# Output projection with u^T stationary and the Wo columns moving, tokens on PSUM rows

## The chip, the cores and the metric

The kernel runs on one core of a Trainium2 chip. Its time is the device time of one execution in microseconds, the median over runs. The engines named below are TensorE (PE, with its weight loads listed apart as PEld), VectorE (DVE), ScalarE (ACT), GpSimd (POOL) and SyncE (SP). SP issues the loads of weights; ACT computes and also issues all other DMAs. Each engine works through its own list of instructions in order.

## The reference

Two branches share the input x (2048 tokens of 640) and are mixed by a gate per token. Branch B is a gated feed-forward layer. Branch A is attention with a recurrent memory: the tokens come in 64 segments of 32, eight memory rows are put ahead of each, and the attention output at the memory rows is the memory of the next segment.

```python
for s in range(n_seg):                       # 64 segments of 32 tokens
    xs = x[:, s * seg_len:(s + 1) * seg_len, :]
    h = jnp.concatenate([mem, xs], axis=1)   # 8 memory rows + 32 tokens
    q, k, v = (einsum('btd,dhe->bhte', h, W) for W in (Wq, Wk, Wv))   # 32 heads of 192
    scores = where(mask, einsum('bhqe,bhke->bhqk', q, k) * scale, -1e9)
    p = softmax(scores)                      # memory rows see all, tokens are causal
    o = einsum('bhqk,bhke->bhqe', p, v)
    o = einsum('bhte,hed->btd', o, Wo)       # the output projection
    mem = o[:, :M, :]
    outs.append(o[:, M:, :])
out = g * a + (1 - g) * b                    # g = sigmoid((x * gate_w).sum(-1))
```

The chain from one segment's memory to the next cannot be broken: Q, K and V of a segment need the memory that the segment before leaves.

## The kernel before

The program is written in Bass. Every operation is put in by `S_.add` with the regions that it reads and writes; from them a small planner works out the semaphore waits (a PSUM bank is one region). The order on each engine is the order of the calls.

Three phases come one after the other. First the feed-forward branch: its rows, already multiplied by 1 - g, are stored to a scratch in HBM (`b_scr`), x is stored transposed (`xts`), and the gates lie in `gcol`, 128 tokens on the partitions and one column for each group of four segments. Then the "left" phase: Q and K of the last eight tokens of every segment, which don't need the memory, are computed for all segments at once and put into a scratch, since 40 rows don't fit into 32. Then the 64 segments, one after the other.

A segment follows the list `PROG` (L463): for each of four octets of heads Q (`q`, `cmode`, L915), its transposition on DVE (`tq`), K, V (`v_oct`, L932), scores (`sc`, L955), softmax (`ex`, L988), transposition of p (`pt`, `p_transp`, L1006), PV (`pv`, `pv_oct`, L1021) and output projection (`wo`, `wo_part`, L1053), interleaved so that TensorE has work while ACT and DVE are at the softmax. In Q, K and V 32 rows (8 memory, 24 tokens) are stationary, in four column tiles of 32, and 384 weight columns move through each. In the output projection it is the other way round: each 128x128 block of Wo is stationary and the 40 columns of u^T move, 48 chunks x 5 blocks = 240 matmuls per segment, all summed up in PSUM bank 7 (`OB`). The result stands transposed: model columns on the partitions and tokens along the row.

What follows on it, at the end of `segment` (L1106 to L1116): ACT copies the eight memory columns into `Hb`, from where the next segment's Q, K and V read them (L1111), and two DVE copies put the other 32 columns into `aT4` (L1113, L1115). After four segments `out_group` (L894) turns `aT4` back by five transposes, mixes it with the rows of branch B in `rowb`, loaded from `b_scr` (L1085), and `out_store` (L902) writes 128 rows.

The weights of branch A, 84 pieces of 384 KB (Wq, Wk, Wv) or 320 KB (Wo), don't all fit into SBUF. As many as fit are resident; two are held in unused corners of PSUM and copied out by ACT (`held2_copy`, L592; `held_copy`, L600); the others are streamed again in every segment through a ring of five slots (`issue_ring`, L546). How many are streamed follows from the bytes that are left (L503 to L511): it is 21. SP issues a streamed piece as soon as the slot that it takes is free.

The names to keep: L920 is the matmul of Q and K, L939 of V, L960 of the mask, L968 of the scores, L1010 and L1011 of `pt`, L1030 to L1042 of PV, L1062 of the output projection, L896 the transposes of `out_group` and L898 its mix. `aux_dma` (L662) is the helper that issues DMAs on ACT.

Of the kernel before, what the change touches and what calls it, by code (L numbers as in the profile page):

```python
# [3 lines left out]
ACTF = mybir.ActivationFunctionType  # L4
# [217 lines left out]
def _build(nc, A_x, A_mem0, A_Wq, A_Wk, A_Wv, A_Wo, seg_len, w_gate, w_up, w_down,  # L222
# [55 lines left out]
    wsA["small"] = al(NG * 4 + 8 + 32 + 16)  # L278
    wsA["ident"] = al(128 * 2)
    wsA["maskm"] = al(R * 2)  # L280
    wsA["rowb"] = al(Dm * 2)
# [12 lines left out]
    wsB["aT4"] = al(KT * 128 * 2)  # L294
# [54 lines left out]
    for k, n in (("gcol", 0), ("mbd", 4 * NG), ("mle", 4 * NG + 8), ("gwT", 4 * NG + 40)):  # L349
        wsA_off[k] = wsA_off["small"] + n  # L350
# [7 lines left out]
    gcol = fview(wsA_off["gcol"], 4 * NG)  # L358
    r_gcol = sreg(wsA_off["gcol"], 4 * NG)
# [15 lines left out]
    rowb = bview(wsA_off["rowb"], Dm * 2)  # L375
    r_rowb = sreg(wsA_off["rowb"], Dm * 2)
# [20 lines left out]
    PTl = bview(wsB_off["PTl"], 256).rearrange("p (i t r) -> p i t r", t=4, r=16)  # L397
# [7 lines left out]
    aT4 = bview(wsB_off["aT4"], KT * 256).rearrange("p (k t) -> p k t", t=128)  # L405
    r_aT4 = sreg(wsB_off["aT4"], KT * 256)
    mem0r = rowb
    r_mem0r = r_rowb
# [178 lines left out]
    HB2 = ((5, 0, 480, 528), (6, 480, 960, 528), (7, 960, 1536, 432))  # L587
# [61 lines left out]
    asel(maskm[:, 0:XA], r_maskm, [[-1, XA]], 0, 1, NEG)  # L649
    asel(maskm[:, L:R], r_maskm, [[-1, M]], -L, 1, NEG)  # L650
    asel(maskm[:, L:R], r_maskm, [[0, M]], -L, 1, 0.0)
    asel(maskm[:, L:R], r_maskm, [[0, M]], -XA, 1, NEG)
# [51 lines left out]

    def chain_init():
        pv7 = psb(7)
        S_.add("pe", [lambda e, k=k: e.transpose(pv7[:, k * M:(k + 1) * M], mem0r[0:M, k * 128:(k + 1) * 128], ident[0:M, 0:M])
                      for k in range(KT)],
               reads=[r_mem0r, r_ident], writes=[r_ps[7]], name="mem0T")
        x_load(0)  # L710
        S_.add("act", lambda e: e.activation(out=Hb[0][:, :, XA:L], in_=pv7[:, 0:KT * M].rearrange("p (k m) -> p k m", m=M),
                                             func=ACTF.Copy),
               reads=[r_ps[7]], writes=[r_Hm[0]], name="mem0T evac")

    def x_load(s):
        nb = s % 2
        aux_dma(Hb[nb].rearrange("p k r -> p (k r)"), xts[s], [Rg("xt", s, s + 1)], [r_Hm[nb], r_Hxp[nb]], "xl")
# [176 lines left out]
    def out_group(g, bk):  # L894
        pv = psb(bk)
        S_.add("pe", [lambda e, k=k: e.transpose(pv[:, k * 128:(k + 1) * 128], aT4[:, k, :], ident) for k in range(KT)],  # L896
               reads=[r_aT4, r_ident], writes=[r_ps[bk]], name="aT transp g%d" % g)
        S_.add("dve", lambda e: e.scalar_tensor_tensor(out=rowb, in0=pv[:, 0:Dm], scalar=gcol[:, g:g + 1], in1=rowb,  # L898
                                                       op0=ALU.mult, op1=ALU.add),
               reads=[r_ps[bk], r_rowb, r_gcol], writes=[r_rowb], name="mix g%d" % g)  # L900

    def out_store(g):  # L902
        aux_dma(out2[128 * g:128 * g + 128, :], rowb, [r_rowb], [], "outw", True)

# [101 lines left out]
    def p_transp(s, o):  # L1006
        bank = 5 + o % 2
        q = s % 4
        pv = psb(bank)
        S_.add("pe", [lambda e: e.transpose(pv[:, 320:424], pm_sb[0:104].rearrange("p t k -> p (t k)"), ident[0:104, 0:104]),  # L1010
                      lambda e: e.transpose(pv[:, 424:528], pl_sb[0:104].rearrange("p t k -> p (t k)"), ident[0:104, 0:104])],  # L1011
               reads=[r_p, r_ident], writes=[r_ps[bank]], name="pT s%d o%d" % (s, o))
        S_.add("dve", lambda e: e.tensor_tensor(  # L1013
            out=PTm, in0=apx(pv[:, 320:424], [[64, 2], [0, 4], [1, R]]), in1=apx(mbd, [[0, 2], [1, 4], [0, R]]),
            op=ALU.mult), reads=[r_ps[bank], r_mbd], writes=[r_PTm], name="pT evac s%d o%d" % (s, o))
        S_.add("dve", lambda e: e.tensor_tensor(  # L1016
            out=PTl, in0=apx(pv[:, 424 + XA:528], [[64, 2], [0, 4], [1, 16]]),
            in1=apx(mle[:, q, :], [[0, 2], [1, 4], [0, 16]]),
            op=ALU.mult), reads=[r_ps[bank], r_mle], writes=[r_PTl], name="pTl evac s%d o%d" % (s, o))

    def pv_oct(s, o):  # L1021
        A, B = misc_bank(), misc_bank()
        v, vl, u = v_sb[o % NVB], vl_sb[o], uT[o % NUB]
        ru = r_uTp[o % NUB]

        def pair(bank, c0, ncol, e0, ia, ib):
            full = ps[:, bank, c0:c0 + ncol]
            n = ib - ia
            part = full.rearrange("p (i t r) -> p i t r", t=4, r=R)[:, :, :, XA:R]
            return [lambda e: e.matmul(full, v[:, e0:e0 + 128], PTm[:, ia:ib], start=True, stop=False,  # L1030
                                       skip_group_check=True),
                    lambda e: e.matmul(part, vl[:, e0:e0 + 128], PTl[:, ia:ib], start=False, stop=True,  # L1032
                                       skip_group_check=True)]

        W = 4 * R
        S_.add("pe", pair(A, 0, W, 0, 0, 1) + pair(A, W, W, 256, 1, 2),
               reads=[r_v[o % NVB], r_vl[o], r_PTm, r_PTl], writes=[r_ps[A]], name="PVa s%d o%d" % (s, o))
        fns = []
        for lhs, pt, left in ((v, PTm, False), (vl, PTl, True)):
            for h in range(2):  # L1040
                dst = ps[64 * h:64 * h + 64, B, 0:W].rearrange("p (t r) -> p t r", r=R)
                fns.append(lambda e, lhs=lhs, pt=pt, left=left, h=h, dst=dst[:, :, XA:R] if left else dst: e.matmul(  # L1042
                    dst, lhs[:, 128 + 64 * h:192 + 64 * h], pt[:, h], start=not left, stop=left,
                    tile_position=(0, 64 * h), skip_group_check=True))
        S_.add("pe", fns, reads=[r_v[o % NVB], r_vl[o], r_PTm, r_PTl], writes=[r_ps[B]], name="PVb s%d o%d" % (s, o))
        S_.add("act", lambda e: e.activation(  # L1046
            out=apx(u[:, 0, 0, :], [[2 * R, 2], [3 * R, 4], [1, R]]),
            in_=ps[:, A, 0:2 * W].rearrange("p (c t r) -> p c t r", t=4, r=R), func=ACTF.Copy),
            reads=[r_ps[A]], writes=[ru[0]], name="uT evac s%d o%d" % (s, o))
        S_.add("dve", lambda e: e.tensor_copy(out=u[:, :, 1, :], in_=ps[:, B, 0:W].rearrange("p (t r) -> p t r", r=R)),  # L1050
               reads=[r_ps[B]], writes=[ru[1]], name="uT mid s%d o%d" % (s, o))

    def wo_part(s, item):  # L1053
        for p in wo_pairs(item):
# [3 lines left out]
            for i in range(2):  # L1058
                c = 2 * p + i
                tl, cc = divmod(c % 12, 3)  # L1060
                for n in range(KT):
                    fns.append(lambda e, g_=g_, i=i, c=c, n=n, tl=tl, cc=cc, u=u: e.matmul(  # L1062
                        ps[:, OB, n * R:(n + 1) * R], g_[:, i, n * 128:(n + 1) * 128], u[:, tl, cc, :],
                        start=(c == 0 and n == 0), stop=(c == NCH - 1), skip_group_check=True))
            S_.add("pe", fns, reads=[rg_, r_uT[(p // WOP) % NUB]], writes=[r_ps[OB]], name="Wo s%d p%d" % (s, p))

    def segment(s):
        g, q = s // 4, s % 4
        for item in PROG:
            kind, i = item[0], item[1]  # L1070
            if kind in ("q", "k"):
# [4 lines left out]
                if kind == "k" and i == 0 and q == 0 and g > 0:  # L1076
                    out_group(g - 1, misc_bank())
                if kind == "k" and i == 1:
                    if q == 0 and g > 0:
                        out_store(g - 1)  # L1080
                if kind == "k" and i == 2:
                    if q == 3:
                        if g + 1 < NG:
                            xleft_load(g + 1)
                        aux_dma(rowb, b_scr[128 * g:128 * g + 128, :], [Rg("dr", 128 * g, 128 * g + 128)], [r_rowb], "rowb")  # L1085
# [22 lines left out]
        O3 = ps[:, OB, 0:KT * R].rearrange("p (n r) -> p n r", r=R)  # L1108
        if s + 1 < NSEG:
            nb = (s + 1) % 2  # L1110
            S_.add("act", lambda e: e.activation(out=Hb[nb][:, :, XA:L], in_=O3[:, :, XA:L], func=ACTF.Copy),  # L1111
                   reads=[r_ps[OB]], writes=[r_Hm[nb]], name="mem evac s%d" % s)
        S_.add("dve", lambda e: e.tensor_copy(out=aT4[:, :, q * L:q * L + XA], in_=O3[:, :, 0:XA]),  # L1113
               reads=[r_ps[OB]], writes=[r_aT4], name="aT evac s%d" % s)
        S_.add("dve", lambda e: e.tensor_copy(out=aT4[:, :, q * L + XA:(q + 1) * L], in_=O3[:, :, L:R]),  # L1115
               reads=[r_ps[OB]], writes=[r_aT4], name="aT evac2 s%d" % s)  # L1116

    xleft_load(0)
# [4 lines left out]
    out_group(NG - 1, misc_bank())  # L1123
    out_store(NG - 1)
# [79 lines left out]
```

## Time and profile before

Time: 1969.43 us, the median of 3 runs (1960.42 to 1974.47). The profiled execution has a span of 1987.3 us.

| what | per run |
|---|---|
| TensorE busy | 1801.4 us (91%), 41036 matmuls |
| weight loads busy | 1179.6 us (59%) |
| DVE busy | 1025.4 us (52%) |
| ACT busy | 813.0 us (41%) |
| POOL busy | 144.7 us (7%) |
| output projection, L1062 | 15360 matmuls of 40 columns |
| Q and K, L920 | 10240 matmuls of 384 columns, in four column tiles |
| V, L939 | 6400 matmuls of 384 columns, in four column tiles |
| DMA | 577.49 MB, mean 291 GB/s |
| weight loads by DMA | 528 of Wo, 404 of Wk, 341 of Wq, 146 of Wv, about 5 us each from issue to landing |
| stores of out | 16 of 160 KB |

The first six slices of the span are the feed-forward branch and the left phase, the rest are the segments. Busy times of TensorE overlap, since the ends of matmuls are modelled: what a stretch of matmuls costs is read from the distance of the starts, not from the mean of one. "Idle before" names what ended an engine's wait, and "issue" stands for time in which it waited for nothing that the profile shows.

### The profile page before, as it was taken

What the parts mean: (1) busy time and instruction counts of PE and PEld (TensorE: products, weight loads), DVE (VectorE), ACT (ScalarE), POOL (GpSimd) and SP (SyncE); (2) the same over time, 40 slices, a digit from 0 to 9 for tenths busy, and PEclk for the clock granted to TensorE, in tenths of its full rate; (3) what the DMA queues carried; (4) which work ended last, traced back from release to release, by engine and by line L of the source; (5) the groups of instructions that cost most, each with busy time, mean ns of one, the idle gap of its engine ahead of it and who ended that gap; (6) DMA issues with size and microseconds to landing.
All of it is one profiled execution on the core that took longest, in us unless ns stands there. A gap on an engine that the chain in (4) does not pass through costs nothing.

```text
span 1987.3 us, 92275 instructions
## 1 busy us (share of the span) xinstructions
PE 1801.4 (91%) x41036; PEld 1179.6 (59%) x41044; DVE 1025.4 (52%) x3164; ACT 813.0 (41%) x1980; POOL 144.7 (7%) x546
## 2 busy tenths in 40 slices
PE   7899996999989999998999899989898999999898
PEld 3454443666666666666666666666665566666665
DVE  3222232555555556565555465555565555555555
ACT  2222221444444444444444444444444444444443
POOL 1000000000000000000000000000000000000000
PEclk9999996999999999999999999999999999999999
DMA  9411569999999999999999999999999999999998
GB/s 372 161 44 64 132 152 331 319 312 316 322 314 315 297 328 314 324 318 313 318 328 317 302 319 335 301 321 312 314 303 306 305 312 321 308 316 325 315 315 283
DMA packets 348330, 577.49 MB, mean 291 GB/s; under 512 B 79506, under 2 KB 232602, under 8 KB 347930
## 3 DMA queue, kind: packets, MB, share of 16 engines
q1 hardware_dynamic: 276922, 531.99, 79.7%
q10 hardware_dynamic: 71008, 39.60, 7.2%
q8 instruction: 320, 5.24, 1.1%
q14 instruction: 80, 0.66, 0.1%
HBM read 550.38 MB, written 21.10 MB: 288 GB/s over the span
## 4 chain that ended last, share of the span: by engine, by line
PE 65%; DMA 26%; issue 4%; ACT 2%; DVE 2%; ACTq 1%; SPq 0%; DVEq 0%
PE ps L920 17%; PE ps L1062 16%; PE ps L939 10%; DMA arena<-in_A_Wq_dram 8%; DMA arena<-in_A_Wo_dram 8%; DMA arena<-in_A_Wk_dram 5%; PE ps L831 5%; DMA arena<-in_A_Wv_dram 3%; PE ps L764 3%; PE ps L761 3%; PE ps L968 3%; PE ps L1042 2%; PE ps L779 2%; PE ps L1030 2%; PE ps L960 1%
## 5 line engine op out<-in xcount | busy, mean ns | idle before, releaser
L920 PE MATMUL ps<-arena 128*32 128x384 bf16 x10240 | 546.2, 335 | 75.7 <-DMA arena<-in_A_Wq_dram 22.5
L1062 PE MATMUL ps<-arena 128*128 128x40 bf16 x15360 | 442.3, 180 | 57.0 <-issue 41.4
L1062 PEld LDWEIGHTS ps<-arena 128*128 128x128 bf16 x15360 | 413.1, 96 | 78.8 <-issue 47.1
L920 PEld LDWEIGHTS ps<-arena 128*32 128x32 bf16 x10240 | 255.0, 98 | 264.6 <-DMA arena<-in_A_Wq_dram 53.3
L924 ACT ACTIVATE arena<-ps 128x384 bf16<-128x384 f32 x512 | 251.4, 491 | 314.6 <-PE ps L920 276.5
L929 DVE STREAM_TRANSPOSE arena<-arena 128x384 bf16<-128x384 bf16 x512 | 292.2, 571 | 115.7 <-ACT arena L924 115.6
L939 PE MATMUL ps<-arena 128*32 128x384 bf16 x6400 | 325.1, 332 | 10.8 <-DMA arena<-in_A_Wv_dram 7.3
L939 PEld LDWEIGHTS ps<-arena 128*32 128x32 bf16 x6400 | 161.7, 98 | 112.8 <-DMA arena<-in_A_Wv_dram 15.1
L950 ACT ACTIVATE arena<-ps 128x384 bf16<-128x384 f32 x256 | 125.7, 491 | 150.3 <-PE ps L939 145.6
L889 POOL COPY arena<-arena 128x96 bf16<-128x96 bf16 x256 | 68.4, 267 | 1628.7 <-PE ps L968 854.1
L1013 DVE TENSOR_TENSOR arena<-ps,arena 128x320 bf16<-128x320 bf16 x256 | 125.2, 489 | 56.0 <-PE ps L1011 50.9
L1046 ACT ACTIVATE arena<-ps 128x320 bf16<-128x320 f32 x256 | 111.6, 436 | 98.3 <-PE ps L1032 97.9
L1113 DVE CAST arena<-ps 128x120 bf16<-128x120 f32 x64 | 18.1, 283 | 256.2 <-ACT arena L1111 252.5
L997 DVE TENSOR_REDUCE arena<-ps 104x4 f32<-104x160 f32 x256 | 81.9, 320 | 123.8 <-ACT ps L995 123.0
L968 PE MATMUL ps<-arena 128*40 128x40 bf16 (+1 forms) x4096 | 120.4, 181 | 1.7 <-issue 0.8
L594 ACT ACTIVATE arena<-ps 128x480 bf16<-128x480 bf16 (+1 forms) x192 | 113.9, 593 | 18.7 <-PE ps L861 16.6
L607 ACT ACTIVATE arena<-ps 128x256 bf16<-128x256 bf16 x320 | 103.7, 386 | 42.2 <-DVE arena L1016 10.9
L983 DVE TENSOR_REDUCE arena<-ps 104x4 f32<-104x160 f32 x256 | 81.2, 317 | 63.0 <-PE ps L968 62.8
L1111 ACT ACTIVATE arena<-ps 128x40 bf16<-128x40 f32 x63 | 12.9, 204 | 246.1 <-PE ps L1062 246.1
L1050 DVE CAST arena<-ps 128x160 bf16<-128x160 f32 x256 | 77.7, 303 | 59.4 <-PE ps L1042 59.1
L968 PEld LDWEIGHTS ps<-arena 128*40 128x40 bf16 (+1 forms) x4096 | 99.7, 96 | 12.6 <-DVE arena L929 1.3
L831 PE MATMUL ps<-arena 128*128 128x512 bf16 x480 | 104.2, 379 | 1.2 <-ACT arena L838 1.2
(75 smaller groups left out, 1712.8 us busy)
## 6 DMA issues: line engine op xcount, KB each, us to landing
arena<-in_A_Wo_dram SPq DMA_DIRECT2D x528, 320.0 KB, 4.8
arena<-in_A_Wk_dram SPq DMA_DIRECT2D x404, 384.0 KB, 5.1
arena<-in_A_Wq_dram SPq DMA_DIRECT2D x341, 384.0 KB, 5.0
arena<-in_A_Wv_dram SPq DMA_DIRECT2D x146, 384.0 KB, 5.1
left_qk_scratch<-arena ACTq DMA_DIRECT2D x16, 768.0 KB, 8.1
arena<-left_qk_scratch ACTq DMA_DIRECT2D x64, 192.0 KB, 4.9
arena<-in_A_x_dram SPq DMA_DIRECT2D x4, 640.0 KB, 15.2
xt_scratch<-arena ACTq DMA_DIRECT2D x4, 640.0 KB, 9.0
```

The costliest lines, as they stand in the source:

```text
L594: S_.add("act", lambda e: e.activation(out=bview(o_held2, GQ)[:, c0:c1], in_=psb(b)[:, p0:p0 + c1 - c0], func=ACTF.Copy), reads=[r_ps[b]], ...
L607: S_.add("act", lambda e, b=b: e.activation(out=flat[:, 256 * b:256 * b + 256], in_=psb(b)[:, 768:1024], func=ACTF.Copy), reads=[r_ps[b]], ...
L831: S_.add("pe", [lambda e, k=k, g_=gs[k][0], i=i, bk=bk: e.matmul(ps[:, bk, 0:NL].rearrange("p (g t) -> p g t", t=L), g_[:, i * 128:(i + 1) ...
L920: S_.add("pe", [lambda e, j=j, k=k, gv=gv: e.matmul(ps[32 * j:32 * j + 32, bank, 0:384].rearrange("p (c i) -> p c i", i=32), Hb[hb][:, k, ...
L924: S_.add("act", lambda e: e.activation(out=rows_sb[m], in_=ps[:, bank, 0:384], func=ACTF.Copy), reads=[r_ps[bank]], writes=[r_rows[m]], na ...
L929: S_.add("dve", lambda e: e.transpose(out=dst[:, :, 0:L], in_=rows_sb[m].rearrange("p (c r) -> p c r", r=L)), reads=[r_rows[m]], writes=[r ...
L939: return [lambda e, j=j: e.matmul(ps[32 * j:32 * j + 32, bk, 0:384], lhs, g_[:, 384 * j:384 * (j + 1)], start=(k == 0), stop=(k == KT - 1) ...
L950: S_.add("act", lambda e: e.activation(out=v_sb[o % NVB], in_=ps[:, bank, 0:384], func=ACTF.Copy), reads=[r_ps[bank]], writes=[r_v[o % NVB ...
L968: fns.append(lambda e, gp=gp, lo=lo, hi=hi, i=3 * tl + c, tl=tl, last=(c == 1): e.matmul(ps[gp:gp + R, bank, tl * R:(tl + 1) * R], Qs[lo:h ...
L1013: S_.add("dve", lambda e: e.tensor_tensor(out=PTm, in0=apx(pv[:, 320:424], [[64, 2], [0, 4], [1, R]]), in1=apx(mbd, [[0, 2], [1, 4], [0, R]]),
L1046: S_.add("act", lambda e: e.activation(out=apx(u[:, 0, 0, :], [[2 * R, 2], [3 * R, 4], [1, R]]), in_=ps[:, A, 0:2 * W].rearrange("p (c t r ...
L1062: fns.append(lambda e, g_=g_, i=i, c=c, n=n, tl=tl, cc=cc, u=u: e.matmul(ps[:, OB, n * R:(n + 1) * R], g_[:, i, n * 128:(n + 1) * 128], u[ ...
```

## The change

The output projection is turned: u^T (128x40) becomes stationary, and Wo moves. Each chunk takes two matmuls of 320 columns, one for each half of the 640 model columns; the halves go to two column tiles of 64, partitions 0 to 39 and 64 to 103 of bank 7. 96 matmuls per segment take the place of 240, and the result stands with tokens on the rows, as `out` and `b_scr` have them. So the transposes of `out_group` and `aT4` go, and each segment is mixed and stored by itself: the gates are spread to a column per segment (`gate_spread`, `gseg`), the rows of B come by two loads per segment (`b_load`), one mix works on both halves, and two stores write it (`out_store`).

The memory, though, is needed with model columns on the partitions. So DVE copies the rows out of PSUM (`mrow`), six small matmuls turn the eight memory rows back (stationary: a piece of `mrow`; moving: eight columns of the identity), and DVE copies the result into `Hb`. The tokens' order in a segment changes with it: the memory comes first, then 24 tokens, then the left eight, so that the 32 tokens are contiguous rows. The mask, the left part of PV (`PTl`) and the load of x (`x_load`) follow this order. The regions of PSUM that hold a weight piece move out of bank 7's first 320 columns (`HB2`), and the transposed p goes to the start of its bank.

```diff
-    wsA["small"] = al(NG * 4 + 8 + 32 + 16)
+    wsA["small"] = al(NSEG * 4 + 8 + 32 + 16)
+    HD = Dm // 2
-    wsA["rowb"] = al(Dm * 2)
+    wsA["rowb"] = al(HD * 2)
+    wsA["mrow"] = al(HD * 2)
-    wsB["aT4"] = al(KT * 128 * 2)
...
-    HB2 = ((5, 0, 480, 528), (6, 480, 960, 528), (7, 960, 1536, 432))
+    HB2 = ((5, 0, 576, 320), (6, 576, 1152, 320), (7, 1152, 1536, 640))
...
+    def gate_spread():
+        S_.add("pool", [lambda e: e.memset(gseg, 0.0), lambda e: e.memset(rowb, 0.0), lambda e: e.memset(mrow, 0.0)],
+               writes=[r_gseg, r_rowb, r_mrow], name="gate zero")
+        for i in range(8):
+            q, h = i % 4, i // 4
+            aux_dma(gseg[64 * h + M:64 * h + R, NG * q:NG * q + NG], gcol[L * q:L * q + L, :], [r_gcol],
+                    [sreg(wsA_off["gseg"] + 8 * i, 8)], "gl%d" % i)
...
-        aux_dma(Hb[nb].rearrange("p k r -> p (k r)"), xts[s], ...
+        aux_dma(Hb[nb].rearrange("p k r -> p (k r)")[:, M:KT * L], xts[s][:, 0:KT * L - M], ...
...
-    def out_group(g, bk):
-        pv = psb(bk)
-        S_.add("pe", [lambda e, k=k: e.transpose(pv[:, k * 128:(k + 1) * 128], aT4[:, k, :], ident) for k in range(KT)],
...
-        S_.add("dve", lambda e: e.scalar_tensor_tensor(out=rowb, in0=pv[:, 0:Dm], scalar=gcol[:, g:g + 1], in1=rowb,
...
             out=PTl, in0=apx(pv[:, 104:208], [[32, 4], [0, 4], [1, M]]),
...
-                for n in range(KT):
-                    fns.append(lambda e, g_=g_, i=i, c=c, n=n, tl=tl, cc=cc, u=u: e.matmul(
-                        ps[:, OB, n * R:(n + 1) * R], g_[:, i, n * 128:(n + 1) * 128], u[:, tl, cc, :],
-                        start=(c == 0 and n == 0), stop=(c == NCH - 1), skip_group_check=True))
+                for h in range(2):
+                    fns.append(lambda e, g_=g_, i=i, c=c, h=h, tl=tl, cc=cc, u=u: e.matmul(
+                        ps[64 * h:64 * h + R, OB, 0:HD], u[:, tl, cc, :], g_[:, i, HD * h:HD * h + HD],
+                        start=(c == 0), stop=(c == NCH - 1), tile_position=(0, 64 * h), skip_group_check=True))
...
-                if kind == "k" and i == 0 and q == 0 and g > 0:
-                    out_group(g - 1, misc_bank())
-                if kind == "k" and i == 1:
-                    if q == 0 and g > 0:
-                        out_store(g - 1)
+                if kind == "k" and i == 0 and s > 0:
+                    out_store(s - 1)
                 if kind == "k" and i == 2:
-                    if q == 3:
-                        if g + 1 < NG:
-                            xleft_load(g + 1)
-                        aux_dma(rowb, b_scr[128 * g:128 * g + 128, :], [Rg("dr", 128 * g, 128 * g + 128)], [r_rowb], "rowb")
+                    b_load(s)
+                    if q == 3 and g + 1 < NG:
+                        xleft_load(g + 1)
...
+        if s + 1 < NSEG:
+            S_.add("dve", lambda e: e.tensor_copy(out=mrow[0:104], in_=ps[0:104, OB, 0:HD]),
+                   reads=[r_ps[OB]], writes=[r_mrow], name="mem rows s%d" % s)
+        S_.add("dve", lambda e: e.scalar_tensor_tensor(out=rowb[0:104], in0=ps[0:104, OB, 0:HD], scalar=gseg[0:104, gx:gx + 1],
+                                                       in1=rowb[0:104], op0=ALU.mult, op1=ALU.add),
+               reads=[r_ps[OB], r_rowb, r_gseg], writes=[r_rowb], name="mix s%d" % s)
         if s + 1 < NSEG:
             nb = (s + 1) % 2
-            S_.add("act", lambda e: e.activation(out=Hb[nb][:, :, XA:L], in_=O3[:, :, XA:L], func=ACTF.Copy),
-                   reads=[r_ps[OB]], writes=[r_Hm[nb]], name="mem evac s%d" % s)
-        S_.add("dve", lambda e: e.tensor_copy(out=aT4[:, :, q * L:q * L + XA], in_=O3[:, :, 0:XA]),
...
-        S_.add("dve", lambda e: e.tensor_copy(out=aT4[:, :, q * L + XA:(q + 1) * L], in_=O3[:, :, L:R]),
...
+            bk = misc_bank()
+            fns = []
+            for k, lo, hi, f0, h in ((0, 0, 128, 0, 0), (1, 0, 128, 128, 0), (2, 0, 64, 256, 0), (2, 64, 128, 0, 1),
+                                     (3, 0, 128, 64, 1), (4, 0, 128, 192, 1)):
+                fns.append(lambda e, k=k, lo=lo, hi=hi, f0=f0, h=h: e.matmul(
+                    ps[lo:hi, bk, k * M:(k + 1) * M], mrow[:, f0:f0 + hi - lo], ident[:, 64 * h:64 * h + M],
+                    start=True, stop=True, skip_group_check=True))
+            S_.add("pe", fns, reads=[r_mrow, r_ident], writes=[r_ps[bk]], name="memT s%d" % s)
+            S_.add("dve", lambda e: e.tensor_copy(out=Hb[nb][:, :, 0:M],
+                                                  in_=ps[:, bk, 0:KT * M].rearrange("p (k m) -> p k m", m=M)),
+                   reads=[r_ps[bk]], writes=[r_Hm[nb]], name="mem evac s%d" % s)
+
+    def b_load(s):
+        for h in range(2):
+            aux_dma(rowb[64 * h + M:64 * h + R, :], b_scr[L * s:L * s + L, HD * h:HD * h + HD],
+                    [Rg("dr", L * s, L * s + L)], [sreg(wsA_off["rowb"] + 2 * h, 2)], "bl%d" % h)
+
+    def out_store(s):
+        for h in range(2):
+            aux_dma(out2[L * s:L * s + L, HD * h:HD * h + HD], rowb[64 * h + M:64 * h + R, :], [r_rowb], [], "ow%d" % h, True)
```

## The prediction

> **What bounds the kernel now.** I read the slices of the span first, then the DMA queues and the chain, then the waits inside the segment phase (400 to 1950 us), and at last single segments, cut from one memory copy (L1111) to the next.
>
> ```profile
> PE   7899996999989999998999899989898999999898
> DMA  9411569999999999999999999999999999999998
> q8 instruction: 320, 5.24, 1.1%
> PE 65%; DMA 26%; issue 4%; ACT 2%; DVE 2%; ACTq 1%; SPq 0%; DVEq 0%
> ```
>
> TensorE and the DMA engines are both nearly full from slice 7 on, and the chain runs through both (65% and 26%). The time is the sum of 64 segments; those from 356.4 to 1958.2 us last 25.84 us each. Windows over single segments:
>
> ```profile
> 1308.55:1334.05 25.50, 22.52 (x592) 15.43 (x592) 13.95 (x46) 11.40 (x29) 2.14 (x8) 1.00 0.95 316
> 1000.57:1024.02 23.45, 22.69 (x592) 15.53 (x592) 14.00 (x46) 11.41 (x29) 2.14 (x8) 1.00 0.98 329
> 1049.86:1075.53 25.67, 25.27 (x677) 17.80 (x677) 16.67 (x51) 11.51 (x29) 2.14 (x8) 1.00 0.95 310
> ```
>
> The columns are length, busy time of PE, its weight loads, DVE, ACT, POOL, then granted clock, DMA share, GB/s. Segments with 677 matmuls (each fourth, with the left V rows) average 27.44 us and the shortest takes 25.55; those with 592 average 25.32, shortest 23.16. So TensorE without stalls needs about (3 x 23.2 + 25.6)/4 = 23.8 us per segment. The DMA side: 21 weight pieces are streamed per segment (8 of 320 KB and 13 of 384 KB, from the issue counts), 7.73 MB, and with the small loads 8.06 MB; the 100-us windows average 315 GB/s at share 0.955, so a full DMA moves 330 and needs 24.4 us. Two limits of 23.8 and 24.4 us, coupled by a ring of five pieces, give 25.84. The waits of TensorE say what separates them:
>
> ```profile
> PEld ps L1062 <- issue: 45.0, 50, 2.3
> PE ps L1062 <- issue: 39.4, 46, 2.2
> PE ps L920 <- ACT arena L1111: 19.3, 59, 0.4
> PE ps L920 <- DMA arena<-in_A_Wq_dram: 18.0, 26, 1.6
> PE ps L1062 <- DMA arena<-in_A_Wo_dram: 11.5, 18, 1.3
> ```
>
> Waits on weight pieces sum to about 50 us, 0.8 us per segment. The "issue" waits (56 us over the segments, 0.9 each, mostly in Wo) wait for nothing the profile names. But from one stall's end to the next the count of matmuls is always a multiple of 128:
>
> ```profile
> 892.70:897.80 5.10, 3.70 (x128) 1.00 0.97 335
> 607.18:612.28 5.10, 3.70 (x128) 1.00 0.95 325
> 1026.68:1048.20 21.52, 20.09 (x512) 1.00 0.98 324
> ```
>
> 128 matmuls with 128 weight loads are 256 instructions: TensorE waits for its own program. Wo is where it eats instructions fastest (80 per us), and its stalls also drop the clock: 14 episodes of some 3.5 us at half clock, 11 of them right after an "issue" stall, cost 24 us of full clock in all.
>
> ```profile
> 1102.00:1103.00 1.00, 0.65 (x22) 0.53 (x18) 0.02 (x1) 0.25 (x2) 0.25 (x1) 0.55 0.94 207
> 1103.00:1104.00 1.00, 1.00 (x16) 0.53 (x20) 0.47 (x2) 0.97 (x2) 0.00 (x0) 0.50 0.61 190
> ```
>
> [...] four 32-column tiles of 384 columns take 0.81 us per five (L920), 0.162 us[...]. [...] the trace shows 0.50 for 3 to 4 slices of 1 us, set off by stalls of 1 to 2 us here. [...] L1062 runs 60 in 1.52 us, 25.3 ns.
>
> **The change part by part, per segment.**
>
> Wo matmuls: 240 of 40 columns at 25.3 ns, 6.07 us, become 96 of 320 columns in pairs on two 64-column tiles. From L920's 0.162 us for 384 columns, 320 take 0.135, and 48 pairs 6.48 us: +0.41. That the two tiles stream together I take from the mask pair (L960): two of 160 columns, on tiles 0 and 64, and the next tile-0 matmul starts 0.08 us later[...]. [...]
>
> Instruction fetch: Wo falls from 480 to 192 instructions in about 6.5 us. A block then lasts 8.7 us instead of 3.2; blocks that stalled came 5.1 us apart. I take 0.8 of the 0.9 us of "issue" away: -0.8 (bounds -0.5 and -0.9).
>
> The boundary. Before, it is one ACT copy:
>
> ```profile
> 1000.57 0.20 ACT L1111 ACTIVATE arena<-ps 128x40 bf16<-128x40 f32 x1 [3.92 <-PE ps L1062]
> 1000.82 0.67 PE L920 MATMUL ps<-arena 128*32 128x384 bf16 x12 [0.29 <-ACT arena L1111]
> ```
>
> Wo ends at 1000.54, so the gap is 0.28 us. After it there are: DVE copy of 104x320 (between L1050's 160 elements, 303 ns, and L953's 384, 547 ns: 477 ns); six matmuls (at the program's end five transposes from DVE's end to DVE's start took 0.61 us at 128 columns; at 8 columns I take 0.45, bounds 0.35 and 0.6); DVE copy of 128x40 (L1115, 200 ns); three handovers of 0.04. But the mix stands ahead of that copy on DVE: 104x320 from PSUM, 489 ns (L1013) to 550 (L898 scaled), so it ends some 0.6 us after the first copy and not 0.46. Behind the memory copy waits the first Q matmul, and behind that the whole segment. Sum 0.04 + 0.48 + 0.60 + 0.20 + 0.04 = 1.36, or +1.08 (bounds +0.9 and +1.4).
>
> DMA issues on ACT: two stores after K0, two loads after K2, each segment. The stores (0.35 us each) delay only the V copy, which has room; they need nothing but the mix, long done. The loads sit ahead of the exponential of octet 1, and wait for the stores to land (5.3 us median, issued some 7 us earlier, so seldom). Where the row load is there today, each fourth segment, it holds TensorE up:
>
> ```profile
> 1034.77 0.44 ACTq L663 DMA_DIRECT2D arena<-ffn_b_scratch  x1
> 1035.26 0.28 ACT L995 ACTIVATE ps<-ps 104x160 f32<-104x160 f32 x1 [0.38 <-issue]
> 1036.65 0.09 PEld L920 LDWEIGHTS ps<-arena 128*32 128x32 bf16 x1 [0.50 <-DVE arena L1002]
> ```
>
> Two issues of 0.33 to 0.44 us do this to two more segments of four (0.45 us each) and 0.35 more to the fourth; the one with the left rows has TensorE work to cover it: +0.3.
>
> Removed: five transposes per four segments (0.39 us), -0.1. The two aT copies (0.48 us of DVE) and the 128x640 mix lay beside Q matmuls: nothing. Token order, mask, PT and held-copy layouts keep counts and dependencies by bank: nothing, hidden where they were. The freed 1,088 bytes don't hold one more piece: 20 streamed pieces need 182,784 bytes resident, the cap rises from 180,608 to 181,696. So streaming stays at 21. Smaller stores and loads carry the same bytes, about 1% of the traffic. Once: eight gate loads and the wait of the left load on them lie beside the resident loads that stall segment 0 anyway, at most +5 us; the end is 1 to 2 us shorter.
>
> Sum on TensorE: 0.41 - 0.8 + 1.08 + 0.3 - 0.1 = +0.9 us per segment, 57 us over 64. The stall-free need becomes 23.8 + 1.7 = 25.5 against 24.4 for DMA. Added TensorE time lets the ring refill and takes away some of the 0.8 us of piece waits and 4.5% of idle DMA costs the rest; I count half as visible, +28 us: 1997 us.
>
> **The rivals.** (1) Nothing is hidden, and the 1.36 us at each boundary sets off the half clock in a third of the segments as stalls of that length do now: 57 + 21 x 1.7 = +93, or +57 without it: about 2045 us, slower. For it: TensorE becomes the larger limit. Against: memory matmuls break the idle time. (2) The other side: the boundary falls where the ring lags, so it only replaces piece waits, while the fetch stalls (0.9 us) and the half clocks (0.37 us per segment) go: with 0.4 us of that visible per segment, -26, 1943 us, faster. For it: DMA's share of 0.95. Against: piece waits are only 0.8 us and spread over the segment. (3) DMA alone sets the pace: bytes don't change, 1969 us.
>
> **How the numbers follow.** Main case 0.4, rival 1 0.2, rival 2 0.2, rival 3 0.2. The main case reaches over +1% (1989 us) in three of four outcomes, so slower 0.4 x 0.75 + 0.2 = 0.5, same 0.28 with most of rival 3, faster 0.22. The range cuts the tails of rivals 1 and 2: 1943 to 2050.
>
> **What would show it.** L1062's successor: 6144 matmuls, 48 pairs in about 6.5 us, no "issue" waits in Wo; "issue" on PE below 15 us over the segments. The gap from the last Wo matmul to the first Q matmul 1.2 to 1.5 us, ended by DVE. Exponential of octet 1 delayed by ACT's DMA issues in every segment. Waits on weight pieces shrink, DMA share to 0.93 or so, mean segment 26.2 to 26.4 us. Wrong would be: pairs at 0.2 us or more, stores that land later than the loads' issue, half clock at many boundaries, or segments that stay at 25.8.

## The result and the profile after

The changed kernel takes 1989.9 us (median of four, 1986.6 to 1995.3) against 1969.8 us: ratio 1.011, 95% interval 1.007 to 1.016. In a second set on another chip it came to 1.012 [1.009, 1.016]. It is slower by a little over 1%; 1997 had been forecast.

The profile of before that the prediction worked from was one of that kernel's longer executions (span 1987.3 us, 18 above the median). The unchanged kernel, profiled again, gave a span of 1969.2, and that trace stands for before below; the second trace of the changed kernel, span 1988.0, stands for after where numbers of the two are set side by side. Each of these is one execution of several.

The page of the changed kernel: the slices of TensorE and of DMA, the instruction queue, and the chain.

```profile
PE   7899994899999999999999999999999999999998
...
DMA  9411468999999999999998999999999999999998
...
q8 instruction: 251, 4.11, 0.8%
...
PE 73%; DMA 14%; DVE 5%; ACTq 5%; ACT 2%; issue 2%; SPq 0%; DVEq 0%
```

Both engines are as full as before, but the chain has moved from DMA (26% to 14%) to TensorE (65% to 73%), to DVE's copies (2% to 5%) and to ACT's DMA issues (ACTq, 1% to 5%). "issue" fell from 4% to 2%, and the instruction queue moved 69 packets fewer (320 to 251). Slice 7 dips to 4 on TensorE, where the page of before has 6; it is the start, below.

The waits of TensorE in the segment phase (400 to 1950 us; columns: us in total, times, longest):

```profile
PEld ps L1119 <- DVE arena L1108: 55.2, 60, 0.9
...
PE ps L1119 <- DVE arena L1108: 35.5, 60, 0.6
...
PE ps L920 <- DVE arena L1123: 20.2, 60, 0.4
...
PE ps L920 <- DMA arena<-in_A_Wq_dram: 9.0, 25, 1.0
PE ps L920 <- DVE arena L1002: 9.0, 24, 1.8
```

The "issue" waits of Wo are gone from the list. In their place are two waits on DVE at every boundary, 35.5 / 60 = 0.59 us for the copy of the memory rows (L1108) and 0.34 us for the copy back into Hb (L1123). One boundary, from the end of Wo to the first Q matmuls (columns: start, us, engine and line, in brackets the idle time before it and what ended that):

```profile
1025.70 3.45 PE L1064 MATMUL ps<-arena 128*40 128x320 bf16 x48
...
1029.19 0.49 DVE L1108 CAST arena<-ps 104x320 bf16<-104x320 f32 x1 [2.96 <-PE ps L1064]
...
1029.60 0.54 DVE L1110 SCALAR_TENSOR_TENSOR arena<-ps,arena 104x320 bf16<-104x320 f32 x1
...
1029.74 0.47 PE L1119 MATMUL ps<-arena 128*128 128x8 bf16 x6 [0.59 <-DVE arena L1108]
1030.32 0.20 DVE L1123 CAST arena<-ps 128x40 bf16<-128x40 f32 x1 [0.17 <-PE ps L1119]
...
1030.57 1.81 PE L920 MATMUL ps<-arena 128*32 128x384 bf16 x40 [0.36 <-DVE arena L1123]
```

From 1029.15 to 1030.57 TensorE does nothing but six matmuls of 8 columns: 1.42 us, which is also the median of 63 boundaries; before, it was 0.35. The mix (L1110) runs while those six matmuls do; it ends at 1030.14, the matmuls at 1030.21, and the copy L1123 begins at 1030.32.

Yet the segments grew little. From the first memory copy to the last, a segment lasts 25.55 us before and 25.72 after: 62 of them make 10.5 us. Another 9.9 lie ahead of the first memory copy (356.4 to 366.3 us), and the end is 1.6 shorter: the +19 of the two traces. Per segment the traces give (the matmuls' spacing and the boundary as medians, the waits and the clock as sums from the first memory copy to the last):

| part | us per segment |
|---|---|
| Wo: a piece every 272 ns, before 251, 24 of them | +0.50 |
| instruction stalls ("issue") | -0.82 |
| half clock (13.7 us of full clock lost before, none after) | -0.22 |
| boundary, 0.35 to 1.42 | +1.07 |
| waits on the softmax (L1002) | +0.17 |
| transposes left out | -0.1 |
| waits on weight pieces | -0.31 |
| sum | +0.29 |
| measured | +0.17 |

0.12 us of the sum is not assigned. The changed kernel's first trace has one episode of half clock in its segments, 1.7 us.

### The profile page after: what moved, and what is told of

Its sections match the earlier page's. It is cut to its first block, busy times and chain, and to the rows that moved or that the text cites. A ratio compares the mean times of both kernels' runs of the same rounds, so it can differ in the third digit from the quotient of the medians.

```text
span 1984.8 us, 74702 instructions
## 1 busy us (share of the span) xinstructions
PE 1833.7 (92%) x32125; PEld 1092.4 (55%) x32125; DVE 1052.9 (53%) x3210; ACT 804.2 (41%) x1917; POOL 146.5 (7%) x547
## 4 chain that ended last, share of the span: by engine, by line
PE 73%; DMA 14%; DVE 5%; ACTq 5%; ACT 2%; issue 2%; SPq 0%; DVEq 0%
PE ps L1064 20%; PE ps L920 18%; PE ps L939 10%; DMA arena<-in_A_Wq_dram 5%; PE ps L842 4%; PE ps L968 3%; DMA arena<-in_A_Wo_dram 3%; PE ps L775 3%; PE ps L772 3%; PE ps L1030 2%; DMA arena<-in_A_Wk_dram 2%; PE ps L1044 2%; PE ps L960 2%; ACTq L666 2%; ACTq L857 2%; PE ps L790 2%
## 5 line engine op out<-in xcount | busy, mean ns | idle before, releaser
L920 PE MATMUL ps<-arena 128*32 128x384 bf16 x10240 | 527.0, 329 | 53.0 <-DVE arena L1123 21.2
L1064 PE MATMUL ps<-arena 128*40 128x320 bf16 x6144 | 466.6, 300 | 4.8 <-DMA arena<-in_A_Wo_dram 3.9
L1064 PEld LDWEIGHTS ps<-arena 128*40 128x40 bf16 x6144 | 297.5, 100 | 102.9 <-DMA arena<-in_A_Wo_dram 9.5
L939 PE MATMUL ps<-arena 128*32 128x384 bf16 x6400 | 318.2, 329 | 12.4 <-DMA arena<-left_xt_scratch 10.0
L599 ACT ACTIVATE arena<-ps 128x576 bf16<-128x576 bf16 (+1 forms) x192 | 114.3, 595 | 224.6 <-PE ps L1064 197.5
L1013 DVE TENSOR_TENSOR arena<-ps,arena 128x320 bf16<-128x320 bf16 x256 | 124.6, 487 | 35.5 <-PE ps L1011 30.7
L1108 DVE CAST arena<-ps 104x320 bf16<-104x320 f32 x63 | 31.0, 492 | 190.1 <-PE ps L1064 190.1
L995 ACT ACTIVATE ps<-ps 104x160 f32<-104x160 f32 x256 | 73.4, 287 | 118.5 <-DVE ps L985 77.2
```

The costliest lines, as they stand in the source:

```text
L599: S_.add("act", lambda e: e.activation(out=bview(o_held2, GQ)[:, c0:c1], in_=psb(b)[:, p0:p0 + c1 - c0], func=ACTF.Copy), reads=[r_ps[b]], ...
L920: S_.add("pe", [lambda e, j=j, k=k, gv=gv: e.matmul(ps[32 * j:32 * j + 32, bank, 0:384].rearrange("p (c i) -> p c i", i=32), Hb[hb][:, k, ...
L939: return [lambda e, j=j: e.matmul(ps[32 * j:32 * j + 32, bk, 0:384], lhs, g_[:, 384 * j:384 * (j + 1)], start=(k == 0), stop=(k == KT - 1) ...
L1013: S_.add("dve", lambda e: e.tensor_tensor(out=PTm, in0=apx(pv[:, 0:104], [[64, 2], [0, 4], [1, R]]), in1=apx(mbd, [[0, 2], [1, 4], [0, R]] ...
L1064: fns.append(lambda e, g_=g_, i=i, c=c, h=h, tl=tl, cc=cc, u=u: e.matmul(ps[64 * h:64 * h + R, OB, 0:HD], u[:, tl, cc, :], g_[:, i, HD * h ...
```

## The experiments

Each expectation stands as it was recorded before the run. Ratios are to the kernel before on the same chip, since its median moved from 1970 to 1977 us between sets. The changed kernel itself was not timed on the chip of the first three of its variants below (gates, row loads, short boundary), so their distance from it is a difference of ratios from two chips.

**The kernel before, again.** No edit.

> The kernel before, unchanged, to get a second profile of it: the first one has a span of 1987.3 us, 18 us above the median time of its runs, so it can't be set against the profile after without care. If that profile was one of many stalls, this one has fewer than 14 half-clock episodes, a mean segment of about 25.5 us and a span near 1968. If the recording itself costs the kernel with 92,000 instructions some 18 us, the span is again near 1987. The time of the runs is 1970 in both.

Ratio 1.0006 [0.9985, 1.0027]; the profiled execution had 8 episodes of half clock where the first had 14, and 25.55 us per segment where the first had 25.84. Its waits on instructions:

```profile
PEld ps L1062 <- issue: 41.0, 50, 1.7
PE ps L1062 <- issue: 35.2, 44, 1.6
```

So the stalls are ordinary (0.82 us per segment), while their number of half-clock episodes varies from execution to execution, and with it the time.

**The start: gates before the left phase.**

```diff
+    gate_spread()
     load_residents(2)
...
-    gate_spread()
     xleft_load(0)
```

> The kernel after, with the eight loads that spread the gates issued before the left phase instead of in front of segment 0. In the profile after they take 9.5 us of ACT's issue, the load of the left x waits for them, and TensorE waits 10 us for it. My theory: this is one fixed cost of some 9 us, 1990 goes to about 1981. Rival: the residents that segment 0 waits for set its end anyway; then the time stays within 3 us of 1990.

What it is to move, from the trace of the changed kernel around 310 us:

```profile
309.32 9.52 ACTq L666 DMA_DIRECT2D arena<-arena  x8
...
322.33 0.34 ACTq L666 DMA_DIRECT2D arena<-left_xt_scratch  x1
...
328.66 3.07 PE L939 MATMUL ps<-arena 128*32 128x384 bf16 x36 [9.97 <-DMA arena<-left_xt_scratch]
```

The eight small gate copies took ACT 9.52 us to issue, 5.04 for the first and 0.61 for each other one; the left load stands behind them, and TensorE waits 9.97 us for it: the dip in slice 7. In the kernel before the left load stood in the first one's place, and its own issue took 4.43 us. With the gates ahead each of the eight takes 0.6 to 0.7 us, the first memory copy comes at 358.8 us instead of 365.5, and the ratio is 1.0066 [1.0045, 1.0088] against 1.011 and 1.012: some 9 us. The intervals just touch or overlap, so the 7 us of the trace are the firmer number. The span of that one profile is no shorter (1985.7 us), since its segments came out longer, 25.81 us.

**The row loads behind the exponential.** One octet later.

```diff
                 if kind == "k" and i == 2:
-                    b_load(s)
...
+                if kind == "k" and i == 3:
+                    b_load(s)
```

> The kernel after, with the two loads of branch B's rows issued on ACT after K3 instead of after K2, so that they no longer stand ahead of the exponential of octet 1. My theory (0.3 us of TensorE time per segment, half of it visible): 1990 goes to about 1980, and the waits of TensorE on the softmax (L1002) fall from 14 us to the 4 us of the kernel before. Rival, DMA sets the pace: 1990 stays within 3 us, since the pieces come no sooner. Rival, nothing of TensorE's time is hidden: 1971.

The changed kernel, ACT's row and an octet's exponential:

```profile
1014.62 0.79 ACTq L666 DMA_DIRECT2D arena<-ffn_b_scratch  x2
...
1015.45 0.28 ACT L995 ACTIVATE ps<-ps 104x160 f32<-104x160 f32 x1 [0.42 <-issue]
...
1016.85 0.09 PEld L920 LDWEIGHTS ps<-arena 128*32 128x32 bf16 x1 [0.50 <-DVE arena L1002]
```

0.79 us of issuing stand ahead of the exponential, and TensorE's weight load waits 0.50 at the end of the chain. The largest of these waits (400 to 1950 us) in the second trace of the changed kernel, and with the loads one octet later:

```profile
PE ps L920 <- DVE arena L1002: 12.7, 30, 1.2
```

```profile
PE ps L920 <- DVE arena L1002: 1.8, 8, 0.3
```

All softmax waits of TensorE fall from 17.4 us to 3.5 in the segments, and the ratio to 1.0019 [1.0001, 1.0037]: 18 to 20 us less by ratios, but 0.15 to 0.19 us per segment, 9 to 12 us, by the segments of the single profiles. Of the 19 us (0.3 x 64) priced for it that is half by the profiles and all by the ratios.

**A short boundary.** Memory rows, transposing matmuls and copy replaced by one ACT copy of 128x40.

```diff
-            S_.add("dve", lambda e: e.tensor_copy(out=mrow[0:104], in_=ps[0:104, OB, 0:HD]),
...
-            S_.add("pe", fns, reads=[r_mrow, r_ident], writes=[r_ps[bk]], name="memT s%d" % s)
...
+            O3 = ps[:, OB, 0:KT * R].rearrange("p (n r) -> p n r", r=R)
+            S_.add("act", lambda e: e.activation(out=Hb[nb][:, :, 0:M], in_=O3[:, :, 0:M], func=ACTF.Copy),
+                   reads=[r_ps[OB]], writes=[r_Hm[nb]], name="mem evac s%d" % s)
```

> The kernel after, with the copy, the six matmuls and the copy at each segment's end replaced by one ACT copy of 128x40 as before; it leaves out turning the memory back, so the next segment gets values from the wrong places. It takes 1.42 - 0.28 = 1.14 us off each of 63 boundaries, 72 us in all. My theory (half of TensorE's added time is visible, the rest turns into waits on weight pieces): 1990 goes to about 1954. Rival, DMA sets the pace: 1980 or more. Rival, TensorE alone sets it: about 1918.

0.9946 [0.9925, 0.9967]; the gap is 0.36 us. Against the changed kernel that is 1.7%, 34 us, of 1.06 x 63 = 67 taken away; by the segments of the single profiles, 25.70 (mean of two) to 25.35, it is 22. The rest shows as waits on weight pieces: 54.0 us in this kernel, 22.3 (second trace) in the changed one. TensorE reaches the pieces earlier and waits for them there. The largest group of these waits, first here, then in the changed kernel:

```profile
PE ps L920 <- DMA arena<-in_A_Wq_dram: 27.7, 57, 2.0
```

```profile
PE ps L920 <- DMA arena<-in_A_Wq_dram: 11.5, 32, 1.3
```

**The mix behind the memory copy.** Its S_.add moved below that of "mem evac".

> The kernel after, with the mix behind the memory copy on DVE and not ahead of it. In the profile after, the memory matmuls end at 1030.28 and the mix at 1030.14, so the copy waits for the matmuls and not for the mix. The profile says: nothing, within 0.2% of the kernel after, and a boundary of 1.42 us as before. My prediction had the mix 0.15 us longer than the matmuls; then each boundary falls by 0.15 us and the time by 5 us.

1.0111 [1.008, 1.0143], beside the changed kernel's 1.0122 on the same chip; the gap is 1.418 us and stays. The mix delays nothing.

**Wo in smaller matmuls.** The same columns, cut in three; 288 matmuls per segment instead of 96.

```diff
-                for h in range(2):
...
+                for lo, hi in ((0, 128), (128, 224), (224, 320)):
+                    for h in range(2):
...
-                        start=(c == 0), stop=(c == NCH - 1), tile_position=(0, 64 * h), skip_group_check=True))
+                            ps[64 * h:64 * h + R, OB, lo:hi], u[:, tl, cc, :], g_[:, i, HD * h + lo:HD * h + hi],
+                            start=(c == 0 and lo == 0), stop=(c == NCH - 1), tile_position=(0, 64 * h), skip_group_check=True))
```

> The kernel after, with each matmul of 320 columns cut into three (128, 96 and 96 columns), so that Wo again has 576 instructions per segment in place of 192 (480 before); the work is the same. Theory: Wo's column time stays 6.5 us (at most 0.3 us more for the spacing), but TensorE eats instructions at 80 per us again, so issue stalls spaced by multiples of 128 matmuls come back, 0.8 us or more per segment, with half-clock episodes; 1990 goes to 2010 to 2030. Rival: the stalls of before belonged [...]to the waits on Wo pieces, not to the number of instructions; then no issue stalls and less than 10 us more.

1.0624 [1.0586, 1.0663], 2096 us: beyond what was expected. The direct cost is small, a piece every 282 ns instead of 272, +0.24 us per segment. The stalls are back:

```profile
PEld ps L1065 <- issue: 65.5, 70, 2.1
...
PE ps L1065 <- issue: 54.1, 62, 1.9
```

and from one to the next there are again 128 matmuls (all 76 distances between the 77 waits in the segments are multiples of 128, give or take two missing records). Stretch after the first wait, and the next wait:

```profile
1652.21 3.18 PE L1065 MATMUL ps<-arena 128*40 128x96 bf16 x128 [0.34 <-issue]
...
1657.32 0.22 PE L1065 MATMUL ps<-arena 128*40 128x96 bf16 x2 [1.94 <-issue]
```

Per segment: 0.24 directly, 1.03 of "issue" (63.7 us over 62 segments), 0.25 of half clock: 1.52 of the 1.74 us by which a segment is longer than in the changed kernel (second trace). The change, then, gained by having fewer instructions, and the stalls come back whole with the instruction count: its weight loads are still 40 columns wide, so weight loads of 128 columns, as the kernel before has them, are not what the stalls need, and the waits on Wo pieces are few here (2.2 us on TensorE).

**The new boundary in the kernel before.** Wo as before; ACT's copy replaced by a DVE copy, six matmuls and a DVE copy of the new kernel's sizes.

```diff
-            S_.add("act", lambda e: e.activation(out=Hb[nb][:, :, XA:L], in_=O3[:, :, XA:L], func=ACTF.Copy),
...
+            S_.add("dve", lambda e: e.tensor_copy(out=mrow, in_=apx(ps[:, OB, 0:160], [[0, 2], [1, 160]])),
...
+            S_.add("pe", fns, reads=[r_mrow, r_ident], writes=[r_ps[bk]], name="memT s%d" % s)
+            S_.add("dve", lambda e: e.tensor_copy(out=Hb[nb][:, :, XA:L],
+                                                  in_=ps[:, bk, 0:KT * M].rearrange("p (k m) -> p k m", m=M)),
```

> The kernel before, with only the new boundary: a DVE copy of 128x320, six small matmuls and a DVE copy of 128x40 in place of the ACT copy of 128x40 (the memory gets wrong values; the rest is as before). It adds about 1.1 us to each of 63 boundaries, 69 us in all, beside the fetch stalls and piece waits of before. My theory of half visible: 35 us more than before, ratio 1.018. Rival, DMA sets the pace: below 1.005. Rival, TensorE sets it: 1.035.

1.0366 [1.0329, 1.0404]: 71 us for a gap of 1.41 instead of 0.35, 1.06 x 63 = 67. Here as much as all of it is visible, where a third to a half was in the changed kernel. A large part of the difference is the clock. A boundary with half clock behind it (here the wait on "issue" next to it is short, 0.23 us), and two windows of 1 us there (columns: length, busy PE, weight loads, DVE, ACT, POOL, granted clock, DMA share, GB/s):

```profile
599.97 0.47 PE L1120 MATMUL ps<-arena 128*128 128x8 bf16 x6 [0.58 <-DVE arena L1114]
...
601.37 0.95 PE L923 MATMUL ps<-arena 128*32 128x384 bf16 x12 [0.23 <-issue]
```

```profile
601.00:602.00 1.00, 0.77 (x13) 0.40 (x16) 0.17 (x1) 0.00 (x0) 0.00 (x0) 0.81 1.00 399
602.00:603.00 1.00, 1.00 (x16) 0.51 (x12) 0.00 (x0) 0.01 (x1) 0.00 (x0) 0.50 0.96 387
```

The clock goes to 0.50. In the segments there are 27 such episodes in this kernel and 52.9 us of full clock lost, against 8 and 13.7 in the kernel before: at most 39 us of the 71 (how much of the half clock fell on time in which TensorE waited was not measured). The granted clocks of all runs of this set agree: over the whole program they leave 83 us of full clock lost here (median of six runs), 37 in the kernel before and 25 in the changed one. The changed kernel has the same boundary and at most one episode in its segments, so the boundary alone doesn't pull the clock down.

It is tempting to say that boundary and instruction stalls together do. The record supports that only in part. Of the 37 boundaries here that have more than 0.3 us of waits on instructions around them (from 5 us before the memory copy to 3 after), 18 come with an episode (it begins at most 1.5 us before the copy or 3 after); of the 26 others still 6. And the kernel with Wo in smaller matmuls has the same boundary and more waits on instructions (63.7 us against 39.2), but 8 episodes, and 41 us of full clock lost in the median of its runs. One thing more that differs is the work ahead of the boundary: here Wo's matmuls of 40 columns, one every 25 ns. No run separates that, so the cause of the half clock stays open. A part of the boundary is hidden here too: waits on weight pieces fall from 41.7 us in the kernel before to 27.9, and those on instructions from 51.3 to 39.2.

**All that can be taken back.** Gates early, loads after K3, the memory rows copied by ACT instead of DVE (438 ns against 490) and the mix last.

```diff
-            S_.add("dve", lambda e: e.tensor_copy(out=mrow[0:104], in_=ps[0:104, OB, 0:HD]),
+            S_.add("act", lambda e: e.activation(out=mrow[0:104], in_=ps[0:104, OB, 0:HD], func=ACTF.Copy),
```

> A version from the findings: the kernel after with the gates spread early, the row loads on ACT after K3, the memory rows copied by ACT (320 columns in 0.44 us, DVE took 0.49) and the mix behind the memory copy on DVE. From 1.0122: gates -0.45%, row loads -0.9%, the copy 0.05 us x 63 = 3 us, at most -0.15%. Expected ratio 0.997, between 0.993 and 1.002; a boundary of 1.37 us.

0.9977 [0.996, 0.9995], 1970.1 against 1974.7 us: just below the kernel before, by less than 0.5%. The boundary is 1.364 us.

**The same with stores and loads issued by SyncE**, stores after K2 and row loads after the scores of the last octet.

```diff
-                if kind == "k" and i == 0 and s > 0:
-                    out_store(s - 1)
                 if kind == "k" and i == 2:
+                    if s > 0:
+                        out_store(s - 1)
...
-                if kind == "k" and i == 3:
-                    b_load(s)
+                if i == NOCT - 1:
+                    b_load(s)
...
-        S_.add(AUXQ, lambda e: e.dma_start(dst, src), reads=reads, writes=writes, dma_sem=sem, watch=watch, name=sem)
+        S_.add(eng, lambda e: e.dma_start(dst, src), reads=reads, writes=writes, dma_sem=sem, watch=watch, name=sem)
```

> The same version, but the stores (after K2) and the row loads (after the scores of octet 3) are issued on SP among the weight pieces, so that ACT issues none of them. If ACT's issue time still costs TensorE something, this is 0.2 to 0.5% below the version with ACT. If not, it is the same. If SP comes to a store or a load before the mix or the landing that it waits for, the weight pieces behind it come late and it is slower: waits on pieces above 40 us.

1.0098 [1.0062, 1.0134]: 1.2% worse than on ACT. SyncE issues the weight pieces, and now two stores and two row loads per segment stand ahead of some of them (the two stores below took 1.04 us). It hardly waited in front of a store or load for anything (once, 1.4 us, from 400 to 1900 us), so it is the issuing itself; the places of the issues moved as well, and what that did is not separated.

```profile
1010.05 1.04 SPq L666 DMA_DIRECT2D out_dram<-arena  x2
...
1011.20 0.36 SPq L556 DMA_DIRECT2D arena<-in_A_Wv_dram  x1
```

Waits on the V pieces (400 to 1900 us), first with SyncE, then with ACT issuing:

```profile
PEld ps L940 <- DMA arena<-in_A_Wv_dram: 19.4, 33, 1.3
```

```profile
PEld ps L940 <- DMA arena<-in_A_Wv_dram: 9.8, 18, 1.1
```

All piece waits of TensorE rise from 38 to 52 us, and the segment from 25.54 to 25.91.

**The floor without the boundary.** The short boundary with gates early and loads after K3.

```diff
+    gate_spread()
     load_residents(2)
...
+                if kind == "k" and i == 3:
+                    b_load(s)
...
+            S_.add("act", lambda e: e.activation(out=Hb[nb][:, :, 0:M], in_=O3[:, :, 0:M], func=ACTF.Copy),
```

> The kernel after without the new boundary (one ACT copy of 128x40, the memory gets wrong values), and with the gates early and the row loads after K3. If DMA is what holds the kernel without the boundary (DMA share 0.96, 54 us of waits on pieces there), the row loads are now worth little: 0.9946 less 0.45% for the gates and less than 0.3% for the loads, about 0.988. If TensorE still sets the pace, they are worth 0.9% again: 0.981.

0.9817 [0.9788, 0.9847], 1934.8 us. Its windows from 400 to 1900 us, and those of the kernel before and the changed one (columns as above):

```profile
400.00:1900.00 1500.00, 1418.31 (x28134) 866.25 (x28130) 879.54 (x2769) 690.09 (x1747) 128.21 (x480) 1.00 0.97 326
```

```profile
400.00:1900.00 1500.00, 1383.80 (x36095) 955.23 (x36099) 863.51 (x2774) 674.52 (x1705) 125.56 (x470) 0.99 0.96 319
```

```profile
400.00:1900.00 1500.00, 1405.34 (x27662) 867.65 (x27654) 886.02 (x2804) 661.73 (x1633) 125.83 (x467) 1.00 0.95 316
```

With the boundary gone, DMA goes up to share 0.97 and 326 GB/s, and a segment takes 24.93 us. Even there, taking away the row loads' wait and the gates' issue is worth 1.3% against the short boundary alone, so TensorE's delays still count at that pace, and the 24.4 us that the prediction took for a full DMA is a limit not yet reached. Against the best version above, on the same chip, it is 35 us less (1970.1 to 1934.8) for 63 boundaries shorter by 1.01 us, 63 us in all: there just over half of the boundary is visible.

## Why the prediction was right, and where it was not

**Wo, +0.41.** The pairs run as forecast: two a piece, 272 ns, 136 ns each against 135. The term measures +0.50 because the old form was quicker than its 25.3 ns per matmul (251 ns for ten, 0.05 us per segment) and the new one a little slower than 135 (another 0.05).

**Instruction fetch, -0.8.** -0.82. The split of Wo shows the cause: more instructions on the same columns bring the stalls back, spaced by 128 matmuls. In the kernel before the waits also stood multiples of 128 matmuls apart, 256 instructions with their weight loads; and the first trace of the changed kernel has 17573 recorded instructions fewer than that of the kernel before (74702 against 92275) and 69 packets fewer on the instruction queue, 255 to a packet. With the old Wo at 80 instructions per us TensorE waited 0.82 us per segment; with the new one at 30 or so its matmuls show no such wait between 400 and 1950 us. Of the 71 waits on instructions before, 23 stood in Q, K and V (12.4 of 51.3 us), which the change leaves as they were; these went too, so a stall need not stand where the instructions are densest.

**Boundary, +1.08.** +1.07: the total is right partly by luck. The forecast had gaps of 0.28 and 1.36 us; they are 0.35 and 1.42 in the median, and the two misses cancel. And the mix, which the forecast let hold up the memory copy for 0.60 us after the first copy, doesn't: it is done after 0.46. The six matmuls and their handovers, forecast at 0.45 and at most 0.6, take 0.63 and fill its place. Moving the mix behind the copy changed nothing, which shows it.

**Row loads ahead of the exponential, +0.3.** The softmax waits grew by 0.17 us per segment on TensorE; moving the loads gives back 9 to 20 us, 0.15 to 0.3 per segment. Right in mechanism; the size is open between half and all of the forecast.

**Half visible.** This step gave nearly the right total and fails as a rule. The parts that the forecast summed to +0.9 come to +0.82 by the table (0.50 - 0.82 + 1.07 + 0.17 - 0.1), so the sum was right; but of it only 0.17 is seen in the segments, a fifth and not half. Shorter waits on weight pieces (-0.31) and the half clock (-0.22), which the main case had put at nothing, gave back most of the rest. Part by part the share differs: of the boundary 22 to 34 of 67 us are visible in the changed kernel, 35 of 63 with the gates early and the row loads later, and 71 of 67 in the kernel before, up to 39 of them the clock; of the loads' wait half or more.

**Mean segment 26.2 to 26.4, DMA share 0.93.** Wrong: 25.7 and 0.95. The forecast added the 28 us to the 25.84 of a longer execution; from the ordinary 25.55 the same step gives 26.0, still too much.

**Startup, at most +5.** Wrong: +9.9. The gates do not lie beside the resident loads without cost: their issue on ACT takes 9.52 us, which was taken as nothing, and it stands ahead of the left load, whose issue ends at 322.7 us and not at 312.7 as before. The end was right: -1.6.

So it is partly luck that the total of +20 is close to +28, since two errors cancel: some 10 us lie in the start, which the total had not taken in, and 10 in the segments, which it priced at 28.

**The rivals.** Half clock at the boundaries (2045) didn't come: at most one episode in the segments. What it described came in the kernel before with the new boundary, 2043 us. The faster side (1943) needs a short boundary, the gates early and the row loads later (1935). Bytes alone (1969) fall with the floor: the same bytes go in 1935 us.

**Open.** 0.12 us per segment of the list, and 0.22 of the split's, have no line. Why the boundary brings half clock in the kernel before and not in the changed one is not separated. Why ACT's first issue behind the stores of the left phase takes 4 to 5 us was not tried.

## What to carry to other kernels

Before a matmul is reshaped, count its instructions per microsecond as well as its columns: at 80 per us TensorE waited 0.8 us per segment for its program, and a form that needed more time per piece, with 40% of the instructions, won that back. Then price what the new layout puts on the serial chain between two stages: here 1.07 us of copies and turning matmuls cost more than the stalls had. A delay was hidden here where another wait (the ring of pieces) lay behind it: of the 67 us of boundary 22 to 34 showed, and without that boundary the waits on pieces were 54.0 us in place of 22.3. So read that wait's total before taking a share as hidden, and issue DMAs neither ahead of an exponential that TensorE waits for (0.79 us of issuing there, 0.50 us of waiting here) nor ahead of the pieces it streams (1.2% here, with the places of the issues moved as well).

## What the hardware showed that was not expected

Half clock came behind waits of 1.0 to 2.2 us, but their length alone does not tell when. In the first trace of the kernel before the clock fell to 0.50 in 14 episodes in the segments, each within 2.3 us of the end of such a wait of TensorE (11 on "issue", 3 on weight pieces), and in the first trace of the changed kernel once, behind 1.85 us on the softmax. Each episode of half clock in the segments lasted 3.4 us or twice that. 63 boundaries of 1.42 us, broken by six small matmuls, gave at most one; the kernel before, with its waits on instructions, had 8 and 14 in two traces; boundary and waits in one kernel gave 27 where Wo ran in matmuls of 40 columns, and 8 where it ran in matmuls of 96 and 128. No single wait of TensorE on instructions or at a boundary in the kernel with 27 was longer than 1.8 us.

The first DMA that ACT issued behind the large stores of the left phase took it 4.43 us in the kernel before, where it was the left load, and 5.04 in the changed one, where it was a small gate copy; the next seven copies took 0.61 each, and a row load in a segment 0.32.
